# Moving the last weight sums of a seven-product matmul stage, and raising one pair of scan products by a place

## The chip, the cores and the metric

The kernel runs on one core of one Trainium2 chip. A core has TensorE (PE, with its weight loads shown apart as PEld), VectorE (DVE), ScalarE (ACT), GpSimd (POOL) and SyncE (SP, which here only issues transfers). The metric is the device time of one execution in microseconds; lower is better. The kernel before took 369.37 us (median of three executions, 368.46 to 369.98). The profiled execution took 368.5 us, and its profile spans 366.8 us; all points of time below are counted from the start of that span.

## The reference

Two blocks follow each other: a chunked state-space scan, and a feed-forward block with an ELU. Cut to what matters here:

```
# scan: x (4, 8, 768, 32), a (4, 8, 768), B and C (4, 8, 768, 16), float32
for c in range(24):                           # chunks of 32 tokens
    y_intra = (C B^T * decay, causal) @ x     # inside the chunk
    y_inter = (C @ state) * decay_to_i        # from earlier chunks
    state   = decay_full * state + sum_j B_j x_j decay_from_j
# bridge: (batch, head, token, d) -> 3072 tokens x 256
h = y @ w_in                                  # 256 -> 2048
g = where(h > 0, h, exp(min(h, 0)) - 1)       # ELU
out = g @ w_out                               # 2048 -> 256
```

## The kernel before, in words

**Blocks.** The 3072 tokens are cut into 12 blocks of 256, numbered n = 0 to 11 in the order of work. The scan of a block ends with products from earlier chunks (`across`, L522) and inside a chunk (`inside`, L542); ScalarE copies their result into `yT`, the left factor of the first feed-forward layer. Two blocks can go through `across` and `inside` together; the table `ends` (L959) says at which step of which block that happens, and `end_of_two` (L961) does it and then calls `sum_y`.

**Blocks 0 to 3** go one at a time. `l1(n, i)` (L577) is one eighth i of the first layer, `l2(n, j)` (L696) one eighth of the second. `elu` (L598) is two passes of ScalarE (L596, L603) and one of VectorE (L605) on a 128x512 tile. For block 3, eighth i, the loop emits, in this order: `l2(1, i)`, `end_of_two(3, 2i)`, `l1(3, i)`, `elu`, one eighth of the weights' sums, `scan_ahead`, `end_of_two(3, 2i+1)`.

**Blocks 4 to 11** go two at a time with a scheme of Strassen's kind: seven products of half size and some sums take the place of eight products, in both layers. It needs sums ahead of the products:

- sums of the weights: `sum_weights` (L621), four `tensor_tensor` of 128x128 per eighth and layer, all recorded as L627. `more_sums(i)` (L1010) does eighth i: the four of `w_out` on VectorE, the four of `w_in` on GpSimd, and `sum_t1(2, i)` (L721, recorded as L723), a subtraction on 128x256 between the two blocks' activations, on VectorE. Before the change, `more_sums(0)` to `more_sums(6)` stand in eighths 1 to 7 of block 3, and `more_sums(7)` stands in the second group of the stage below.
- sums of the scan's results: `sum_y(n)` (L641, recorded as L646), four subtractions on 128x256 on GpSimd, one reading another's result.
- sums of the activations for the second layer: `sum_t2` (recorded as L719) and the subtractions inside `second` (also L719), on GpSimd.

**A stage by two blocks** is a loop over 16 half steps k, i = k // 2; here called eight *groups* i = 0 to 7. The stage of blocks 4 and 5 carries the second layer of blocks 2 and 3 along in `steps = second(2)`, a generator of 56 steps, one 128x128x256 product each; `l2s(c)` takes c of them. The order on TensorE's queue in a group is:

```
front(n, i)        3 products   L651; ACT copies the first one (L661)
l2s(2), l2s(2)     4 products   L753
mid(n, i)          2 products   then DVE L678 reads the second one
l2s(2)             2 products
back(n, i)         2 products   the first writes where L678 has read
l2s(1)             1 product
```

`front_sums` (L669, L670), the sum of `mid` (L678) and those of `back` (L685, L686) are 128x256 sums on VectorE; then two `elu` of the group follow. VectorE and GpSimd also collect the second layer's results whenever four of its products are done: `add` in `second` (L745). At the end of its fourth sum (r == 3) GpSimd forms `p5 = p5 + u`; at the end of the fifth (r == 4, the 20th step, in the third group) VectorE adds that p5 to a product. `scan_ahead` puts work for the next two blocks between: in the stage of blocks 4 and 5 two masks of GpSimd (L444, `affine_select`) in the second group and two in the third, and `turn` with `turn_exp` (four transposes on TensorE, L381 and L389 on VectorE) after the third and the fourth group.

The order is written out by hand (`manual_schedule`): every engine executes its instructions in the order in which the program emits them. Tiles come from rotating pools (seven PSUM banks of pool `ps_a`, one of `ps_o`).

Of the kernel before, what the change touches and what calls it, by code (L numbers as in the profile page):

```python
# [28 lines left out]
def kernel(  # L29
# [27 lines left out]
    nc = tc.nc  # L57
# [29 lines left out]
    for k in range(4):  # L87
        (nc.scalar if k % 2 else nc.sync).dma_start(
            out=la0[BH * k:BH * (k + 1)],
# [142 lines left out]
    for v in range(2):  # L232
        nc.gpsimd.affine_select(
            out=low16[Q * v:Q * v + Q], in_=low16[Q * v:Q * v + Q], pattern=[[1, Q]],
# [5 lines left out]
        out=hmask, in_=hmask, pattern=[[-N, NH]], compare_op=ALU.is_ge, fill=0.0,  # L240
        base=0, channel_multiplier=1)
    nc.gpsimd.affine_select(
        out=hmask, in_=hmask, pattern=[[N, NH]], compare_op=ALU.is_ge, fill=0.0,
# [8 lines left out]
        out=minus, in0=ident, scalar1=-1.0, scalar2=None, op0=ALU.mult)  # L252
# [178 lines left out]
    def decay(n, q):  # L431

        decay_of(n, 2 * q)
        decay_of(n, 2 * q + 1)
# [142 lines left out]
    def l1(n, i):  # L577

        ps = psum([P, 2, BLK], "ps_h")
        for j in range(2):  # L580
            m = 2 * i + j
            for k in range(KC):
                nc.tensor.matmul(  # L583
                    out=ps[:, j], lhsT=w_in[:, k, m * P:(m + 1) * P],
                    rhs=yT[n // 2][:, k, n % 2].rearrange("p u i -> p (u i)"),
                    start=(k == 0), stop=(k == KC - 1))
        lag.append((n, i, ps))
# [31 lines left out]


    def sum_weights(eng, a, s, i):  # L621
        a11, a12, a21, a22 = (part[:, i] for part in a)
        s2, s3, s4 = (part[:, i] for part in s)
        for out, in0, in1, op in (
                (s3, a11, a21, ALU.subtract), (a21, a21, a22, ALU.add),
                (s2, a21, a11, ALU.subtract), (s4, a12, s2, ALU.subtract)):
            eng.tensor_tensor(out=out, in0=in0, in1=in1, op=op)  # L627

    def weight_sums():
        return [conv.tile([P, MC // 2, P], F32, tag="w64", name="w_sum", bufs=W_AHEAD)  # L630
# [3 lines left out]
    a_in = a11, a12, a21, a22 = [w_parts[:, k, r] for r in range(2) for k in range(2)]  # L634
    w_parts = w_out.rearrange("p (i k) (r c) -> p k r i c", k=2, c=P)
    a_out = [w_parts[:, k, r] for r in range(2) for k in range(2)]
    s_in, s_out = [], []
# [12 lines left out]
    def part_product(out, lhsT, rhs, first=False):  # L650
        nc.tensor.matmul(  # L651
            out=out, lhsT=lhsT, rhs=rhs, start=first, stop=True, skip_group_check=True)
# [27 lines left out]
    def back(n, i):  # L680
        c1, c2, u = open_.pop((n, i))
        b22 = yT[n // 2][:, 1, 1].rearrange("p u i -> p (u i)")
        part_product(c1[:, 1], a22[:, i], y_sums[n][:, 3])
        part_product(c2[:, 0], s_in[2][:, i], b22)
        nc.vector.tensor_tensor(out=c1[:, 1], in0=c1[:, 1], in1=u[:, 0], op=ALU.add)  # L685
        nc.vector.tensor_tensor(out=c2[:, 0], in0=c2[:, 0], in1=u[:, 0], op=ALU.add)  # L686
        lag.append((n, i, c1))
        lag.append((n + 1, i, c2))
# [7 lines left out]
    def l2(n, j, half=None):  # L696


        if j == 0 and half != 1:
            o_of[n] = p_o.tile([P, 2, DM], F32, tag="o", name="ps_o")  # L700
        for m in (2 * j, 2 * j + 1) if half is None else (2 * j + half,):
            for ts in range(2):
                nc.tensor.matmul(  # L703
                    out=o_of[n][:, ts], lhsT=g_of[n, j][:, m % 2, ts * P:(ts + 1) * P],
                    rhs=w_out[:, m], start=(m == 0 and ts == 0), stop=(m == MC - 1),
                    skip_group_check=True)
        if j == MC // 2 - 1 and half != 0:
            ob = ffn.tile([P, 2, DM], F32, tag="ob", name="ob")
            nc.scalar.copy(out=ob, in_=o_of.pop(n))
            r0 = row_of(n)  # L710
            nc.sync.dma_start(
                out=out[r0:r0 + BLK, :].rearrange("(t p) e -> p t e", p=P), in_=ob)
# [5 lines left out]
    def sub(out, in0, in1):  # L718
        nc.gpsimd.tensor_tensor(out=out, in0=in0, in1=in1, op=ALU.subtract)  # L719

    def sum_t1(n, i, eng=nc.gpsimd):  # L721
        b12 = g_of[n + 1, i][:, 0]
        eng.tensor_tensor(out=b12, in0=b12, in1=g_of[n, i][:, 0], op=ALU.subtract)  # L723

    def sum_t2(n, half):
        for i in range(4 * half, 4 * half + 4):
            t2_of[n, i] = ffn.tile([P, BLK], F32, tag="t2", name="t2", bufs=4)
            sub(t2_of[n, i], g_of[n + 1, i][:, 1], g_of[n + 1, i][:, 0])
# [80 lines left out]
    def w_take(i, low):  # L809

        w_abs(i)
        w_low(i, low)
        w_sign(i)

    def w_give(i):

        w_high(i)
        w_sum(i)
# [137 lines left out]

    ends = {(3, 14): (4, 5), (4, 12): (6, 7), (6, 12): (8,), (6, 14): (9,), (8, 13): (10, 11)}  # L959

    def end_of_two(n, step):  # L961
        ns = ends.get((n, step))
        if ns:
            inside(across(*ns), *ns)
            if ns[-1] % 2:
                sum_y(ns[-1] - 1)
# [43 lines left out]
    def more_sums(i):  # L1010
        sum_weights(nc.vector, a_out, s_out, i)
        sum_weights(nc.gpsimd, a_in, s_in, i)
        sum_t1(2, i, nc.vector)


    for n in (2, 3):
        for i in range(8):
            l2(n - 2, i)
            if todo < len(pieces):
                w_take(todo, nc.vector)  # L1020
            end_of_two(n, 2 * i)
            l1(n, i)
            if todo < len(pieces):
                w_give(todo)
                w_load(todo + 6)
                todo += 1
            while lag:
                elu()
            if n == 2:
                if i < 2:  # L1030
                    decay(3, 2 * i)
                    decay(3, 2 * i + 1)
                if i == 1:
                    scaled(3, nc.gpsimd)
                    turn(3)
                    turn_exp(3)
                if i == 2:
                    scores(3)
                    for q in range(4):
                        weigh(3, q)  # L1040
                if i == 4:
                    sums(3)
                    states(3)
                if i == 6:
                    inside(across(3), 3)
            else:
                if i == 0:
                    s_in[:], s_out[:] = weight_sums(), weight_sums()
                else:
                    more_sums(i - 1)  # L1050
            scan_ahead(n, i)
            end_of_two(n, 2 * i + 1)
    sum_t2(2, 0)

    for n in range(4, NP, 2):
        m = n + 2 if n + 2 < NP else None
        steps = second(n - 2)

        def l2s(count):
            for _ in range(count):  # L1060
                next(steps)

        def next_elu():
            if lag:
                at = lag[0][:2]
                elu()
                if at[0] % 2:
                    sum_t1(at[0] - 1, at[1])

        for k in range(16):  # L1070
            i = k // 2
            if k % 2 == 0:
                if m and i == 5:
                    l2s(3)
                    next_elu()
                    weigh_two(m, 1)
                    sums(m, m + 1)
                    front(n, i)
                    weigh_two(m, 2)
                    front_sums(n, i)  # L1080
                    weigh_two(m, 3)
                else:
                    front(n, i)
                    front_sums(n, i)
                    next_elu()
                    if n == 4 and i == 1:
                        more_sums(7)
                    l2s(2)
                    end_of_two(n, k)
                    l2s(2)  # L1090
            elif m and i == 5:
                l2s(2)
                mid(n, i)
                states(m)
                l2s(2)
                back(n, i)
                states(m + 1)
                next_elu()
                begin_elu()
            else:  # L1100
                mid(n, i)
                if i == 0 and n > 4:
                    store(n - 4, turn_out(n - 4, 0))
                    store(n - 3, turn_out(n - 4, 1))
                l2s(2)
                back(n, i)
                l2s(1)
                next_elu()
                begin_elu()
            if m:  # L1110
                scan_ahead(n + k // 8, k % 8)
                if k == 9:
                    scores(m, m + 1)
                    weigh_two(m, 0)
                if k % 2:
                    end_of_two(n, k)
        for _ in steps:
            pass
    next_elu()

    n = NP - 2
# [50 lines left out]
```

## Time and profile before

| engine | busy us | share of the span |
|---|---|---|
| PE (matmul) | 355.7 | 97% |
| PEld (weight load) | 299.3 | 82% |
| DVE | 244.8 | 67% |
| POOL | 226.4 | 62% |
| ACT | 207.0 | 56% |

The granted TensorE clock was 1.000 over the whole span. "Busy" of PE contains modelled ends of pipelined matmuls, so what TensorE loses is better read from gaps in front of its weight loads. In the stages in question a product of 128x128x256 shows as two weight loads and two matmuls; two such products advance the queue by 0.86 us, so one is worth 0.43 us. The whole seam between block 3 and the third group of the first stage by two lies between 107 and 140 us, and the lines on it are shown with the prediction.

### The profile page before, as it was taken

The page shows a single profiled execution, that of the slowest core. Times are in us where ns is not written, and L with a number is a line of the kernel's source. Part 1 is how long each engine was busy: PE and PEld are TensorE (multiplying, and loading weights), DVE is VectorE, ACT ScalarE, POOL GpSimd, SP SyncE. Part 2 cuts the span into 40 slices and gives each one's busy share as a digit, 9 for nine tenths or more (in the row PEclk, how much of TensorE's full clock was granted, in tenths as well). Part 3 has the DMA queues.
Part 4 walks back from the last instruction along what each step waited for, and adds up shares of the span by engine and source line. Part 5 has one row for each costly group of instructions (what it writes and reads, how often), then busy time and mean ns, then how long its engine had stood idle before and what let it go on. Part 6 is the DMA issues. An engine that isn't in the chain of part 4 may idle for free.

```text
span 366.8 us, 9144 instructions
## 1 busy us (share of the span) xinstructions
PE 355.7 (97%) x3458; PEld 299.3 (82%) x3458; DVE 244.8 (67%) x550; ACT 207.0 (56%) x515; POOL 226.4 (62%) x364
## 2 busy tenths in 40 slices
PE   8899999999999889999999999999999999999995
PEld 5578878888888778788888778888888888888884
DVE  3989978972795777785567784566784566656212
ACT  4859969766336466644686645486735452535101
POOL 4454544654376886679366678558579545464972
PEclk9999999999999999999999999999999999999999
DMA  8979895561053430063260063151000010000101
GB/s 152 229 198 224 218 243 140 61 126 33 3 116 57 57 61 1 5 122 39 66 92 2 3 119 43 45 86 30 2 2 2 22 37 0 3 0 0 61 0 57
DMA packets 96252, 25.27 MB, mean 69 GB/s; under 512 B 77328, under 2 KB 92112, under 8 KB 96208
## 3 DMA queue, kind: packets, MB, share of 16 engines
q1 hardware_dynamic: 94032, 24.49, 32.2%
q8 instruction: 27, 0.44, 0.5%
q10 hardware_dynamic: 2176, 0.20, 0.4%
q14 instruction: 17, 0.14, 0.1%
HBM read 21.33 MB, written 3.34 MB: 67 GB/s over the span
## 4 chain that ended last, share of the span: by engine, by line
PE 87%; DVE 7%; ACT 2%; POOL 1%; issue 1%; DVEq 0%; POOLq 0%; ACTq 0%
PE ps_o L753 31%; PE ps_h L651 25%; PE ps_h L583 14%; PE ps_o L703 8%; PE ps_y L553 2%; PE ps_g L459 2%; PE ps_t L796 1%; PE ps_y L534 1%; DVE g L605 1%; PE ps_st L489 1%; PE ps_idle L215 1%; ACT e L596 1%; DVE mag L183 1%; DVE mag L190 1%; ACT e L603 1%
## 5 line engine op out<-in xcount | busy, mean ns | idle before, releaser
L596 ACT ACTIVATE e<-ps_h 128x512 f32<-128x512 f32 x96 | 56.4, 588 | 87.8 <-DVE ps_h L685 66.6
L605 DVE SCALAR_TENSOR_TENSOR g<-e,ps_h 128x512 f32<-128x512 f32 x96 | 65.2, 682 | 41.7 <-ACT e L603 41.6
L753 PE MATMUL ps_o<-g,w_out 128*128 128x256 f32 x320 | 79.6, 380 | 0.0
L753 PEld LDWEIGHTS ps_o<-g,w_out 128*128 128x128 f32 x320 | 60.2, 190 | 8.5 <-issue 0.5
L723 POOL TENSOR_TENSOR g<-g 128x256 f32<-128x256 f32 x32 | 23.3, 727 | 69.3 <-DVE g L605 69.3
L583 PE MATMUL ps_h<-yT,w_in 128*128 128x256 f32 x256 | 60.7, 383 | 2.3 <-ACT w_in L164 1.4
L603 ACT ACTIVATE e<-e 128x512 f32<-128x512 f32 x96 | 60.9, 634 | 2.1
L583 PEld LDWEIGHTS ps_h<-yT,w_in 128*128 128x128 f32 x256 | 47.7, 190 | 10.5 <-POOL w_in L200 3.0
L753 PE MATMUL ps_o<-g,w_sum 128*128 128x256 f32 x160 | 42.1, 380 | 0.0
L651 PE MATMUL ps_h<-y_sum,w_in 128*128 128x256 f32 x128 | 38.6, 383 | 2.7 <-DVE ps_h L678 2.6
L439 ACT ACTIVATE L<-L,ncum 128x64 f32<-128x64 f32 x160 | 41.0, 338 | 0.0
L651 PE MATMUL ps_h<-y_sum,w_sum 128*128 128x256 f32 x128 | 38.5, 382 | 0.4 <-DVE g L605 0.2
L651 PE MATMUL ps_h<-yT,w_in 128*128 128x256 f32 x128 | 38.5, 382 | 0.0
L444 POOL TENSOR_SCALAR_AFFINE_SELECT L<-L 64x512 f32<-64x512 f32 x40 | 27.4, 685 | 12.6 <-ACT L L439 11.3
L753 PEld LDWEIGHTS ps_o<-g,w_sum 128*128 128x128 f32 x160 | 30.2, 190 | 4.3 <-DVE g L605 0.2
L703 PE MATMUL ps_o<-w_out,g 128*128 128x256 f32 x128 | 30.7, 382 | 0.0
L651 PEld LDWEIGHTS ps_h<-y_sum,w_in 128*128 128x128 f32 x128 | 23.5, 189 | 7.9 <-DVE ps_h L678 3.1
L719 POOL TENSOR_TENSOR g<-t,g 128x256 f32<-128x256 f32 x40 | 27.8, 729 | 1.1 <-PE ps_o L753 1.1
L719 POOL TENSOR_TENSOR t<-g 128x256 f32<-128x256 f32 x40 | 28.1, 735 | 0.3
L651 PEld LDWEIGHTS ps_h<-y_sum,w_sum 128*128 128x128 f32 x128 | 23.9, 190 | 5.1 <-issue 0.9
L719 POOL TENSOR_TENSOR g<-g,t 128x256 f32<-128x256 f32 x40 | 27.8, 725 | 0.2
L685 DVE TENSOR_TENSOR ps_h<-ps_h,u_sum 128x256 f32<-128x256 f32 x32 | 13.7, 430 | 20.4 <-PE ps_h L651 20.3
(114 smaller groups left out, 558.1 us busy)
## 6 DMA issues: line engine op xcount, KB each, us to landing
L<-flat SPq DMA_DIRECT2D x20, 256.0 KB, 4.6
w<-in_moe_w_in_dram SPq DMA_DIRECT2D x8, 512.0 KB, 5.0
w<-in_moe_w_out_dram SPq DMA_DIRECT2D x8, 512.0 KB, 6.3
xr<-in_x_dram SPq DMA_DIRECT2D x24, 128.0 KB, 3.6
out_dram<-ob SPq DMA_DIRECT2D x11, 256.0 KB, 2.2
bc<-in_B_dram SPq DMA_DIRECT2D x24, 64.0 KB, 3.9
bc<-in_C_dram SPq DMA_DIRECT2D x22, 64.0 KB, 3.3
ec<-flat_exp SPq DMA_DIRECT2D x72, 16.0 KB, 1.7
```

Source lines behind the costliest of these rows:

```text
L439: nc.scalar.activation(L[:, h, u], L[:, h, u], ACT.Exp, bias=ncum[:, u, row:row + 1])
L444: nc.gpsimd.affine_select(out=part, in_=part, pattern=[[0, 4], [0, 2], [1, Q]], compare_op=ALU.is_ge, fill=0.0, base=0, channel_multiplier=-1)
L583: nc.tensor.matmul(out=ps[:, j], lhsT=w_in[:, k, m * P:(m + 1) * P], rhs=yT[n // 2][:, k, n % 2].rearrange("p u i -> p (u i)"), start=(k = ...
L596: nc.scalar.activation(begun[0], lag[0][2], ACT.Relu, scale=-1.0)
L603: nc.scalar.activation(e, e, ACT.Exp, scale=-1.0)
L605: nc.vector.scalar_tensor_tensor(out=g_of[n, i], in0=e, scalar=1.0, in1=ps, op0=ALU.subtract, op1=ALU.max)
L651: nc.tensor.matmul(out=out, lhsT=lhsT, rhs=rhs, start=first, stop=True, skip_group_check=True)
L685: nc.vector.tensor_tensor(out=c1[:, 1], in0=c1[:, 1], in1=u[:, 0], op=ALU.add)
L703: nc.tensor.matmul(out=o_of[n][:, ts], lhsT=g_of[n, j][:, m % 2, ts * P:(ts + 1) * P], rhs=w_out[:, m], start=(m == 0 and ts == 0), stop=( ...
L719: nc.gpsimd.tensor_tensor(out=out, in0=in0, in1=in1, op=ALU.subtract)
L723: eng.tensor_tensor(out=b12, in0=b12, in1=g_of[n, i][:, 0], op=ALU.subtract)
L753: nc.tensor.matmul(out=ps, lhsT=a[:, i], rhs=b, start=(i == chunk[0]), stop=(i == chunk[-1]))
```

## The change

It does three things, all around that seam.

1. `inside(across(4, 5))` with `sum_y(4)` stood at step 14 of block 3, between `l2(1, 7)` and `l1(3, 7)`. It is put at step 13, so at the end of eighth 6, ahead of `l2(1, 7)`. The sums that the first group needs are to be ready when it starts.
2. `more_sums(6)` leaves the end of block 3, and `more_sums(7)` leaves the second group. VectorE's eight sums of `w_out` for these two eighths (four each) are handed out two at a time behind `back` in each of the groups 0, 1, 2 and 3.
3. GpSimd's four sums of `w_in` for eighth 6 come behind `back` of group 0, those of eighth 7 behind `back` of group 1. `sum_t1(2, 6)` and `sum_t1(2, 7)` go with them, on GpSimd where they were on VectorE.

No arithmetic is added or dropped.

```
     def sum_weights(eng, a, s, i):
+        for step in weight_steps(eng, a, s, i):
+            step()
+
+    def weight_steps(eng, a, s, i):
...
-            eng.tensor_tensor(out=out, in0=in0, in1=in1, op=op)
+            yield lambda: eng.tensor_tensor(out=out, in0=in0, in1=in1, op=op)
...
-    ends = {(3, 14): (4, 5), (4, 12): (6, 7), (6, 12): (8,), (6, 14): (9,), (8, 13): (10, 11)}
+    ends = {(3, 13): (4, 5), (4, 12): (6, 7), (6, 12): (8,), (6, 14): (9,), (8, 13): (10, 11)}
...
                 if i == 0:
                     s_in[:], s_out[:] = weight_sums(), weight_sums()
-                else:
+                elif i < 7:
                     more_sums(i - 1)
...
     sum_t2(2, 0)
+    left = (step for i in (6, 7) for step in weight_steps(nc.vector, a_out, s_out, i))
...
                     next_elu()
-                    if n == 4 and i == 1:
-                        more_sums(7)
                     l2s(2)
...
                 back(n, i)
+
+                if n == 4 and i < 4:
+                    for _ in range(2):
+                        next(left)()
+                    if i < 2:
+                        sum_weights(nc.gpsimd, a_in, s_in, 6 + i)
+                        sum_t1(2, 6 + i)
                 l2s(1)
                 next_elu()
                 begin_elu()
```

## The prediction

> **What bounds the kernel now.** TensorE. On the page's first part PE is busy 355.7 of 366.8 us, and its part 4, the chain that ended last, begins:
>
> ```profile
> PE 87%; DVE 7%; ACT 2%; POOL 1%; issue 1%; DVEq 0%; POOLq 0%; ACTq 0%
> ```
>
> So a change is worth what it takes out of TensorE's queue or out of its waits. The next view is busy time by stretches (columns: stretch and its length, then PE, PEld, DVE, ACT, POOL busy, clock, DMA share, GB/s). I cut it where the weight load of each group's `front` starts, so the rows are groups 0 to 3 of the stage of blocks 4 and 5:
>
> ```profile
> 116.70:124.64 7.94, 6.55 (x29) 5.16 (x28) 5.14 (x11) 1.91 (x5) 7.51 (x13) 1.00 0.48 52
> 124.64:132.37 7.73, 6.32 (x30) 5.24 (x29) 5.85 (x14) 4.77 (x14) 5.94 (x10) 1.00 0.49 75
> 132.37:138.41 6.04, 6.04 (x29) 5.31 (x28) 4.12 (x10) 4.40 (x13) 5.24 (x9) 1.00 0.23 36
> 138.41:144.94 6.53, 6.53 (x33) 5.63 (x32) 4.71 (x12) 4.67 (x14) 4.96 (x8) 1.00 0.00 1
> ```
>
> Group 2 is the undisturbed one: 14 products in 6.04 us, 0.43 us each. Row 4 contains about 0.5 us of transposes and otherwise the same 6.0. Groups 0 and 1 exceed 6.04 by 1.90 and 1.69 us, **3.59 us together**. The weight-load timeline says where (in brackets the idle time ahead and its releaser):
>
> ```profile
> 117.67 0.30 PEld L651 LDWEIGHTS ps_h<-y_sum,w_sum 128*128 128x128 f32 x2 [0.56 <-POOL y_sum L646]
> ...
> 123.45 0.30 PEld L651 LDWEIGHTS ps_h<-y_sum,w_in 128*128 128x128 f32 x2 [1.60 <-POOL t L719]
> ...
> 131.18 0.30 PEld L651 LDWEIGHTS ps_h<-y_sum,w_in 128*128 128x128 f32 x2 [1.82 <-DVE ps_h L678]
> ```
>
> The first is `front(4, 0)` waiting for `sum_y`. The second and third are `back` of groups 0 and 1. The matmul of the second waits on DVE L678 (its own record says 1.23 us for that), the POOL name being only the last event seen. They add up to 3.98 us; the groups lost 3.59, since loads after a gap follow closer (0.32 us instead of 0.43). I use 3.59. VectorE's timeline shows why L678 is late in group 0:
>
> ```profile
> 118.41 0.69 DVE L605 SCALAR_TENSOR_TENSOR g<-e,ps_h 128x512 f32<-128x512 f32 x1 [3.73 <-ACT e L603]
> 119.01 0.54 DVE L627 TENSOR_TENSOR w_sum<-w_out 128x128 f32<-128x128 f32 x1
> ...
> 121.06 0.94 DVE L723 TENSOR_TENSOR g<-g 128x256 f32<-128x256 f32 x1
> 121.93 0.41 DVE L669 TENSOR_TENSOR u_sum<-ps_h,p_copy 128x256 f32<-128x256 f32 x1
> ...
> 122.91 0.43 DVE L678 TENSOR_TENSOR ps_h<-ps_h,u_sum 128x256 f32<-128x256 f32 x1
> ```
>
> `more_sums(6)` stands ahead of `front_sums`, from 119.01 to 121.93. In group 1 `more_sums(7)` does the same from 128.09 to 130.38.
>
> **What the Trainium skill says.** "PSUM — Partial Sum Buffer", section Engine vs sequencer instructions: the queues of ScalarE, VectorE and GpSimd are strict FIFO. The trace agrees: L669 had its input at 118.63 and started at 121.93, when the sums ahead of it were done. "SBUF — State Buffer", section Who interferes with whom: a VectorE instruction with two SBUF inputs contends with a GpSimd one that reads SBUF. The trace agrees: an L627 on VectorE takes 0.28 us at 128.09 with GpSimd idle and about 0.50 beside its sums. "Perfetto Trace Analysis", section GPSIMD Engine Instruction: time GpSimd by the spacing of starts. L627 there lasts 0.45 us by its record, but starts come 0.53 apart; I use spacings.
>
> **The change, part by part.**
>
> *Scan products up.* On TensorE only the order changes, cost nothing. `l2(1, 7)` is 8 loads, 1.73 us (110.77 to 112.5), so `inside`, the copies of `yT` and `sum_y` come 1.73 us earlier. The second result of `sum_y` was used at 117.67; 1.73 earlier is 115.9, ahead of 117.1 where TensorE asks. The 0.56 us gap closes. The copy of block 1's output, now behind the `yT` copies, ends near 115.9 instead of 113.5; the bank is needed at 118.0 and the transfers queued behind it on SP are used after 134, so nothing waits.
>
> *Sums out of VectorE ahead of L678.* With `front(4, 0)` at 116.70 undisturbed: 3 products to 118.0, 4 to 119.7, `mid` to 120.6, L678 ready at 121.0. VectorE has L605 to 119.0, L669 and L670 to 120.0, so it is waiting there. In group 2 L678 ends (137.10) just where `back` wants to start (137.16): there is no slack, and any lateness of VectorE is a gap on TensorE. Here there is none; both long gaps close.
>
> *Two sums behind each `back`.* After L686 VectorE waited 0.89, 0.90 and 1.00 us for ACT (groups 0 to 2) and 0.47 in group 3. Two L627 at 0.45 to 0.50 fill 0.9 to 1.0, so L605 is late by 0.1 at most in groups 0 to 2. In groups 1 and 2 VectorE stands 0.35 to 0.4 us ahead of L678. In group 3 the excess of 0.1 to 0.5 meets 0.42 us of idle time ahead of the next L678. Cost: nothing on the path.
>
> *GpSimd.* The same eight L627, and two L723 at 0.69 spacing that VectorE did in 0.41 and 0.94. They now stand in the middle of the stage's GpSimd work, while TensorE comes earlier. Two lines of before are the measure:
>
> ```profile
> 136.74 0.72 POOL L745 TENSOR_TENSOR p_sum<-p_sum 128x256 f32<-128x256 f32 x1
> ...
> 137.60 0.42 DVE L745 TENSOR_TENSOR c_sum<-ps_o,p_sum 128x256 f32<-128x256 f32 x1 [0.50 <-PE ps_o L753]
> ```
>
> The second needs the first and product r == 4; both were there near 137.5. After the change, groups start at 116.70, 122.74 and 128.78, so r == 4 is done at 128.78 + 5.13 = 133.9. GpSimd: `sum_y` to 117.2, four L719 to 120.0, four more from 120.2 to 123.0, eighth 6 (4 x 0.53) to 125.1, L723 to 125.8. The next L723 needs the second `elu` of group 0, which came 3.54 us after the front of group 1, so 126.35. From there without a pause: L723 0.69, four L719 2.77, two masks 1.38, eighth 7 2.1, two L723 1.38, the p5 sum 0.72, together 9.04: 135.4. VectorE gets it at 135.55 instead of 134.0: **late by 1.55 us**. Behind that add on VectorE are L685, L686, the `elu`s, `turn`'s two, `front_sums` and L678 of group 3. Before, VectorE ran without a gap from 140.02 to that L678 at 143.28, where it was already 0.17 us behind the product. Nothing absorbs it: `back` of group 3 waits some 1.55 us, less 0.1 for the closer loads: **1.45 us given back**. After it GpSimd catches up in pauses of 1.43 and 4.24 us (before L723 at 143.10 and 149.41), and the groups from 4 on only move.
>
> *Sum.* 369.37 - 3.59 + 1.45 = **367.2 us**. The unseen resource is the backlog on GpSimd. Its lower bound is zero (365.8). For an upper one, every L627 on GpSimd at its longest 0.72 instead of 0.53 adds 8 x 0.19 = 1.5: 368.7. I take the middle, for which I have every duration.
>
> **Rivals.** *All of it comes in, 365.8 us*: GpSimd keeps up, group 3 runs in 6.5. For it: its pauses of before (1.55 us at 126.7) are filled first. Against: the 9.04 us run above fits in no way into the 7.5 us from 126.35 to 133.9. *Half of the likely gain, 368.4 us*: port conflicts stretch two L627 behind each `back` from 0.9 to 1.4 us (0.71 was seen once), VectorE misses L678 by 0.1 to 0.2 in groups 1 and 2, and GpSimd's lag grows by 0.8; together 1.2 more. For it: VectorE and GpSimd overlap much more here. *Slower, 370.1 us*: the bound becomes GpSimd for the whole first half, and a 1.45 us wait comes back in three groups, 4.35 in all against 3.59 gained, 0.76 net. Against: pauses in groups 3 and 4 sum to 5.67 us.
>
> **How the numbers follow.** Likely case 0.50, full gain 0.25, half 0.17, slower 0.08. Faster by over 0.5% means below 367.52: about 0.7 of the first case (0.35), all of the second, little of the third (0.03): 0.63. Within: 0.15 + 0.13 + 0.02 = 0.30. Slower 0.07. Runs of before scatter by 0.7 us around the median. With that, 365.3 to 368.8 reaches to both neighbouring cases and leaves out the slower one and the edges.
>
> **What would show it.** In the profile after: no PEld wait on L646 and none over 0.2 us on L678 in groups 0 and 1, which are 6.0 us long; L627 of VectorE in pairs between L686 and L605; the DVE L745 of r == 4 waiting for POOL L745; group 3 some 1.5 us longer, its `back` waiting for L678. I am wrong if group 3 stays at 6.5 us (then 365.8), or if L678 is late in groups 1 and 2 too.

## The result, and the profile after

The changed kernel took **365.81 us** (median of 4 executions, 365.62 to 366.49) against 368.99 us of the kernel before measured along with it: ratio **0.9914, 95% interval 0.9888 to 0.9941**, 2.2 to 4.1 us faster. Its profile spans 363.9 us instead of 366.8. The new helper shifts all later lines by four: what was L627, L678, L685, L723, L745 before is L631, L682, L689, L727, L749 after.

The page's part 4, the chain that ended last:

```profile
PE 90%; DVE 6%; ACT 1%; POOL 1%; issue 1%; DVEq 0%; POOLq 0%; ACTq 0%
```

Busy time by stretches, cut at the same instructions as before (columns: stretch and length, then PE, PEld, DVE, ACT, POOL busy, clock, DMA share, GB/s):

```profile
115.97:122.02 6.05, 6.05 (x30) 5.25 (x29) 2.33 (x6) 1.86 (x4) 6.05 (x10) 1.00 0.67 103
122.02:128.06 6.04, 6.04 (x30) 5.31 (x28) 4.39 (x11) 4.78 (x14) 4.89 (x9) 1.00 0.52 57
128.06:134.10 6.04, 6.04 (x29) 5.31 (x28) 4.53 (x9) 4.40 (x13) 5.66 (x11) 1.00 0.64 101
134.10:142.06 7.96, 7.02 (x33) 5.54 (x32) 6.41 (x16) 4.67 (x14) 6.56 (x10) 1.00 0.01 3
```

The lengths are the reading: groups 0 and 1 fell from 7.94 and 7.73 us to 6.05 and 6.04; the row of group 3 rose from 6.53 to 7.96. From the front of group 0 to the front of group 4, which I call *the seam*, it is 26.64 us (115.97 to 142.61) where it was 28.79 (116.70 to 145.49): 2.15 us less. From there to the end both profiles need 221.3 us. The other 0.73 us between the two spans lies ahead of the first changed instruction, and the experiments come back to it.

The weight-load timeline of groups 0 to 3 has two waits left, both in group 3:

```profile
138.18 0.30 PEld L655 LDWEIGHTS ps_h<-yT,w_in 128*128 128x128 f32 x2 [0.65 <-ACT p_copy L665]
...
140.88 0.30 PEld L655 LDWEIGHTS ps_h<-y_sum,w_in 128*128 128x128 f32 x2 [1.10 <-DVE ps_h L682]
```

The first is `mid`, waiting for ScalarE's copy, the second `back`, waiting for VectorE's L682. Where VectorE lost its time shows on GpSimd's timeline, at the p5 sum, and on its own:

```profile
133.97 0.72 POOL L749 TENSOR_TENSOR p_sum<-p_sum 128x256 f32<-128x256 f32 x1
```

```profile
132.36 0.43 DVE L682 TENSOR_TENSOR ps_h<-ps_h,u_sum 128x256 f32<-128x256 f32 x1
134.72 0.42 DVE L749 TENSOR_TENSOR c_sum<-ps_o,p_sum 128x256 f32<-128x256 f32 x1 [1.93 <-PE ps_tb L374]
...
140.40 0.42 DVE L682 TENSOR_TENSOR ps_h<-ps_h,u_sum 128x256 f32<-128x256 f32 x1
```

VectorE stands still for 1.93 us ahead of the add of r == 4 and starts it 0.03 us after GpSimd's p5 sum ends (133.97 + 0.72). The name in the bracket, a transpose of TensorE, is only the last event before; the add doesn't read it. A releaser's name has to be held against what the instruction reads. From the add at 134.72 to L682 at 140.40 the profile shows no further wait of VectorE, so `back` of group 3 is late by what the add is late.

### The profile page after: what moved, and what is told of

Same layout as the page of the kernel before. It is cut to its first block, busy times and chain, and to the rows that moved or that the text cites. A ratio compares the mean times of both kernels' runs of the same rounds, so it can differ in the third digit from the quotient of the medians.

```text
span 363.9 us, 9138 instructions
## 1 busy us (share of the span) xinstructions
PE 354.9 (98%) x3458; PEld 299.1 (82%) x3458; DVE 243.5 (67%) x548; ACT 207.0 (57%) x515; POOL 227.5 (63%) x366
## 4 chain that ended last, share of the span: by engine, by line
PE 90%; DVE 6%; ACT 1%; POOL 1%; issue 1%; DVEq 0%; POOLq 0%; ACTq 0%
PE ps_o L757 32%; PE ps_h L655 26%; PE ps_h L583 14%; PE ps_o L707 8%; PE ps_y L553 2%; PE ps_g L459 2%; PE ps_t L800 1%; PE ps_y L534 1%; PE ps_st L489 1%; PE ps_idle L215 1%; DVE g L605 1%; DVE mag L183 1%; DVE mag L190 1%; PE ps_tb L374 1%; PE ps_tc L374 1%
## 5 line engine op out<-in xcount | busy, mean ns | idle before, releaser
L727 POOL TENSOR_TENSOR g<-g 128x256 f32<-128x256 f32 x34 | 24.7, 727 | 67.7 <-DVE g L605 67.7
L723 POOL TENSOR_TENSOR g<-t,g 128x256 f32<-128x256 f32 x40 | 27.8, 728 | 1.1 <-PE ps_o L757 1.1
L723 POOL TENSOR_TENSOR t<-g 128x256 f32<-128x256 f32 x40 | 28.0, 732 | 0.2
L723 POOL TENSOR_TENSOR g<-g,t 128x256 f32<-128x256 f32 x40 | 27.9, 728 | 0.3
L689 DVE TENSOR_TENSOR ps_h<-ps_h,u_sum 128x256 f32<-128x256 f32 x32 | 13.8, 430 | 20.4 <-PE ps_h L655 20.4
```

## The experiments

The ten experiments were each timed in five rounds beside the kernel before on the same chip (e1 to e4 on one, e5 to e7 on a second, e8 to e10 on a third), and each leaves a profile. Two measures are given: the ratio of the times, and the seam in the profile. Of the same kernel the seam comes out the same within 0.02 us, so it is the finer one for anything that happens inside it. It is blind to what happens behind it: from the front of group 4 to the kernel's last two loads of a transpose (L796 before, L800 after) TensorE needs 217.25 to 217.28 us in eight of the twelve profiles, but 217.32 in e5, 217.36 in e8, 217.52 in e6 and 217.55 in e7. The groups in the table run from front to front, so group 2 contains the transposes (6.59 us undisturbed).

| kernel | groups 0, 1, 2, 3, us | seam, us | median, us | ratio (95% interval) |
|---|---|---|---|---|
| before | 7.94, 7.73, 6.59, 6.53 | 28.79 | 368.99 | 1 |
| changed | 6.05, 6.04, 6.59, 7.96 | 26.64 | 365.81 | 0.9914 (0.9888 to 0.9941) |
| e1: scan products up, alone | 8.42, 7.73, 6.58, 6.53 | 29.26 | 369.87 | 1.0032 (1.0019 to 1.0044) |
| e2: sums moved, alone | 6.47, 6.04, 6.59, 8.46 | 27.56 | 367.94 | 0.9966 (0.9953 to 0.9980) |
| e3: GpSimd's sums later | 6.04, 6.04, 6.59, 6.65 | 25.32 | 365.71 | 0.9912 (0.9893 to 0.9932) |
| e4: changed, again | 6.04, 6.04, 6.59, 7.96 | 26.63 | 367.15 | 0.9949 (0.9932 to 0.9967) |
| e5: p5 sum on VectorE | 6.05, 6.04, 7.00, 6.48 | 25.57 | 366.41 | 0.9913 (0.9885 to 0.9941) |
| e6: no pair in group 2 | 6.04, 6.04, 6.59, 7.96 | 26.63 | 367.47 | 0.9947 (0.9928 to 0.9965) |
| e7: e3, no pair in group 1 | 6.04, 6.05, 6.58, 6.84 | 25.51 | 366.50 | 0.9929 (0.9902 to 0.9957) |
| e8: e3, no pair in groups 1, 2 | 6.04, 6.05, 6.58, 6.54 | 25.21 | 365.70 | 0.9900 (0.9870 to 0.9930) |
| e9: e3, again | 6.04, 6.05, 6.58, 6.67 | 25.34 | 365.90 | 0.9904 (0.9873 to 0.9935) |
| e10: changed, a third time | 6.05, 6.04, 6.59, 7.97 | 26.65 | 367.55 | 0.9939 (0.9921 to 0.9958) |

The kernel before, timed along with e1 to e4, e5 to e7 and e8 to e10, had medians of 368.95, 369.18 and 369.40 us.

### The parts one by one (e1, e2)

e1 is the kernel before with one edit:

```
-    ends = {(3, 14): (4, 5), ...
+    ends = {(3, 13): (4, 5), ...
```

> The kernel before, with the scan products of blocks 4 and 5 one place up and nothing else. Theory of the chain: L678 of group 0 ends at a time that VectorE sets (second elu of block 3 at 118.4, then 2.9 us of weight sums, then front_sums), so closing the 0.56 us gap at sum_y only makes the gap ahead of back longer by as much. Groups 0 and 1 stay at 15.6 to 15.7 us from the front of group 0 to that of group 2, total within 0.3 us of before (ratio 0.999 to 1.001). Rival, parts that add up: the gap at sum_y is worth its own 0.45 to 0.56 us, total 0.5 us less than before (ratio 0.9986).

Measured: seam 29.26 us, 0.47 *longer* than before, and 0.3% slower. The gap at `sum_y` is gone, as expected; the next gap takes it and more. Its weight-load line for `back` of group 0, and two of VectorE's sums ahead of L678:

```profile
125.61 0.30 PEld L651 LDWEIGHTS ps_h<-y_sum,w_in 128*128 128x128 f32 x2 [2.51 <-POOL g L719]
```

```profile
121.14 0.70 DVE L627 TENSOR_TENSOR w_out<-w_out 128x128 f32<-128x128 f32 x1
121.87 0.70 DVE L627 TENSOR_TENSOR w_sum<-w_out 128x128 f32<-128x128 f32 x1
```

The gap grew from 1.60 to 2.51 us, by 0.91. Some 0.43 of that is the closed gap, net of the closer loads behind it, as expected: VectorE and not TensorE sets the end of L678. The other 0.48 comes from VectorE itself: three of its four sums take 0.70 us here instead of 0.49 to 0.50, because GpSimd, released earlier, is by now in its 128x256 subtractions (four from 120.92) instead of its short sums; the stretch from the first sum to L669 is 3.40 us instead of 2.92. That this is GpSimd's doing rests on the times lying side by side and on the same slowing in other places; no run changes GpSimd alone here. My expected 0.3 us bound was broken; the rival, a gain of 0.5, is ruled out. The ratio puts the loss at 1.2 us (0.7 to 1.6), more than the seam does. The new order on TensorE isn't the rest: from the last `l1` ahead of the moved products to the front of group 0 it needs 7.65 us, and 7.66 before. The rest stays open.

e2 is the changed kernel with that edit undone.

> The changed kernel, with the scan products of blocks 4 and 5 put back to step 14. Theory of the chain: the gap of 0.56 us at sum_y in group 0 comes back (0.45 net), and GpSimd starts its run 1.7 us later, which the pauses of GpSimd ahead of the L723 of group 0 take up but for about 0.4, so that the p5 sum comes 0.4 us later against TensorE and group 3 grows by as much: 0.85 us slower than the changed kernel, some 1.3 us of gain left by the seam. Rival, parts that add up: 0.45 us slower than the changed kernel. Other rival, the early scan products do nothing: same as the changed kernel.

Measured: seam 27.56 us, 0.92 more than the changed kernel (0.85 expected): 0.42 in group 0, where the gap of 0.56 us at `sum_y` is back, and 0.50 in group 3, where the p5 sum ends 7.13 us after the front of group 2 (6.63 in the changed kernel). Ratio 0.9966, a gain of 1.25 us; 1.23 by the seam. So the scan products' move is worth 0.92 us with the sums moved and -0.47 without. The larger half of the 0.92 isn't at the gap that it closes; it comes from GpSimd's earlier start, paid out three groups later.

### What makes group 3 long (e3, e5, e6)

e3 moves only GpSimd's weight sums, out of groups 0 and 1:

```
                     if i < 2:
-                        sum_weights(nc.gpsimd, a_in, s_in, 6 + i)
                         sum_t1(2, 6 + i)
+                    else:
+                        sum_weights(nc.gpsimd, a_in, s_in, 4 + i)
```

> The changed kernel, with GpSimd's sums of w_in for the last two eighths behind back of groups 2 and 3 instead of groups 0 and 1; the two sums of activations stay. This takes 4.2 us from GpSimd ahead of the p5 sum. Theory that the p5 sum is late: it now starts as soon as its inputs are there, the VectorE add of r == 4 waits 0.2 us at most for it, both gaps in group 3 (0.65 and 1.10 us of weight-load idle in the changed kernel) close, group 3 goes from 7.96 back to about 6.5 us, total 1.4 us less than the changed kernel (364.4). Rival, the two extra VectorE sums behind back are what makes L678 late in group 3: group 3 stays near 7.9 us and the total at 365.8.

Measured: group 3 6.65 us instead of 7.96, seam 1.32 us shorter than that of the changed kernel (1.4 expected). Total 365.71 us against 367.15 of the changed kernel on the same chip, 1.44 less. The rival falls. VectorE's add still waits for p5, but the line now names GpSimd and a third of the time:

```profile
134.82 0.42 DVE L749 TENSOR_TENSOR c_sum<-ps_o,p_sum 128x256 f32<-128x256 f32 x1 [0.62 <-POOL p_sum L749]
```

Most of those 0.62 us are TensorE's. In the kernel before, where the add waited 0.50 us for its product, it started 5.23 us after the front of group 2 (137.60 - 132.37). Here it starts 5.36 us after it (134.82 - 129.46), so p5 holds it for 0.13 us, less than the 0.2 expected. One short wait of 0.30 us on L682 is left in group 3.

e5 leaves GpSimd's load alone and takes the p5 sum from it:

```
-                    add(p5, p5, u)
+                    if n == 2 and not half:
+                        nc.vector.tensor_tensor(out=p5, in0=p5, in1=u, op=ALU.add)
+                    else:
+                        add(p5, p5, u)
```

> The changed kernel, with the p5 sum of the third group on VectorE (0.42 us) instead of GpSimd; GpSimd's load ahead of it is left as it is. Theory that VectorE's add of r == 4 waits for GpSimd: it now starts at 133.3 instead of 134.7 (as counted in the changed kernel), group 3 falls from 7.96 to 6.5 or 6.6 us, while the extra 0.42 us ahead of L678 of group 2 costs 0.2 to 0.5 us there. From the front of group 0 to that of group 4 25.4 to 25.7 us against 26.64. Rival, GpSimd's load slows VectorE through the shared port, whoever does the p5 sum: group 3 stays above 7.5 us and the total at that of the changed kernel.

Measured: group 3 6.48 us, group 2 7.00 (0.41 more), seam 25.57, all as expected. The rival falls. On VectorE the sum took 0.67 us beside GpSimd's sums, and L682 of group 2 came that late:

```profile
134.53 0.67 DVE L776 TENSOR_TENSOR p_sum<-p_sum 128x256 f32<-128x256 f32 x1
135.12 0.42 DVE L682 TENSOR_TENSOR ps_h<-ps_h,u_sum 128x256 f32<-128x256 f32 x1
```

```profile
135.59 0.30 PEld L655 LDWEIGHTS ps_h<-y_sum,w_in 128*128 128x128 f32 x2 [0.55 <-DVE ps_h L682]
```

With e3 this shows the cause from two sides: relieve GpSimd ahead of the p5 sum, or take the sum off GpSimd, and group 3 is short again, with the same sums done in the same stage.

e6 takes VectorE's pair out of group 2 and puts it behind `back` of group 4.

> The changed kernel, with no VectorE pair of weight sums behind back of group 2; the pairs go behind back of groups 0, 1, 3 and 4. Theory: the pair lies beside ScalarE's two passes and costs nothing, group 3 stays at 7.9 to 8.0 us, from front of group 0 to front of group 4 26.6 us. Rival, the pair makes L678 of group 3 late: group 3 falls to 7.0 us or less, as the pair took 1.0 us there.

Measured: 7.96 us for group 3, seam 26.63, no change; the rival falls. The line of the first `elu` behind `back` of group 2 shows what the pair had stood in:

```profile
139.19 0.69 DVE L605 SCALAR_TENSOR_TENSOR g<-e,ps_h 128x512 f32<-128x512 f32 x1 [0.99 <-ACT e L603]
```

Without the pair VectorE waits 0.99 us for ScalarE there; with it, it works for 1.02 and waits for nothing. In group 2 the pair was free, as costed.

In its new place behind `back` of group 4, past the end of the seam, it was not:

```profile
150.91 0.59 DVE L631 TENSOR_TENSOR w_sum<-w_out 128x128 f32<-128x128 f32 x1
151.53 0.70 DVE L631 TENSOR_TENSOR w_sum<-w_out,w_sum 128x128 f32<-128x128 f32 x1
152.16 0.68 DVE L605 SCALAR_TENSOR_TENSOR g<-e,ps_h 128x512 f32<-128x512 f32 x1
```

It took 1.25 us (150.91 to 152.16) where VectorE waits 0.89 us for ScalarE in the changed kernel. TensorE comes to the second product of the front of group 5 10.56 us after the front of group 4 instead of 10.31, and keeps this 0.25 us to the end. Of the other profiles only e7, which has a pair in this place too, is late there by as much (10.61).

### How much is the gain (e4, e9, e10)

> The changed kernel once more, unaltered, for the size of the gain. From the front of group 0 to that of group 4 the profiles give 28.79 us before and 26.64 after, 2.15 us; the rest of the 2.9 us between the two profiled spans lies ahead of the first changed instruction (0.44 us ahead of 20 us, 0.28 near 51 us). Theory that this rest is scatter of the start: the ratio comes out at 0.993 to 0.995 (1.8 to 2.6 us), and the front of group 0 varies by some tenths from run to run. Rival, it belongs to the change: ratio 0.991 to 0.992 again (2.9 us or more) and the front of group 0 at 116.0 again.

> The kernel with GpSimd's weight sums behind back of groups 2 and 3, once more, unaltered. If the length from front of group 0 to front of group 4 is what the change decides, it is 25.3 us again, and the ratio to before lies 0.003 to 0.004 below that of the changed kernel on the same chip. If its first 365.7 us were luck of the start, the two come out alike.

> The changed kernel a third time, unaltered, beside the two above. Theory: 26.6 us from front of group 0 to front of group 4 again, ratio 0.993 to 0.996 (gain 1.5 to 2.6 us), the front of group 0 anywhere between 116 and 119 us. Rival: ratio 0.991 as in the first measurement.

Measured: the changed kernel's ratio comes out at 0.9949 and 0.9939, gains of 1.9 and 2.3 us (0.0051 x 368.95 and 0.0061 x 369.40); e6, with the same seam, gives 0.9947. The 0.991 of the rivals did not come again, and the seam says 2.15. The first measurement's 0.9914 (3.2 us) rests on four executions. Its interval includes 0.9939 but not 0.9949, and the interval of e4 reaches up to a gain of 2.5 us. The front of group 0 was at 115.97 us in the profile of the first measurement, 118.74 in e4's and 118.02 in e10's, with the same instructions ahead of it. That is far more than the tenths that I expected. From there to the end the three profiles need the same, 247.9 us (363.9 - 115.97 in the first), and the granted clock (0.999, 1.000 and 0.995) doesn't order them. Over all 12 profiles the front lies between these ends, in no order that follows the kernels. In the changed kernel's first profile the 0.73 us that it is ahead of the kernel before came in two pieces: the weight loads of L410 (32 of them) took 0.46 us instead of 0.75 and began 0.14 earlier, and near 51 us a wait ahead of weight loads was 0.33 instead of 0.60. What sets the start apart from run to run was not followed further. So the likely size of the change is the seam's, 2.15 us, and I put 1 us of the first measured 3.2 down to start and scatter.

e9 repeats e3: seam 25.34, ratio 0.9904 beside 0.9939 of the changed kernel, 1.3 us apart by ratio and by seam alike.

### Towards a better version (e7, e8)

e7 is e3 with VectorE's pairs behind `back` of groups 0, 2, 3 and 4.

> GpSimd's weight sums behind back of groups 2 and 3 (as in the experiment that did this alone), and VectorE's pairs behind back of groups 0, 2, 3 and 4, none in group 1, where the pair took 1.45 us beside GpSimd's masks. Theory: the second elu of group 1 then ends about 0.4 us earlier, the p5 sum on GpSimd, which waits for the L723 behind that elu, too, and the last wait on L678 in group 3 (0.27 us of weight-load idle) closes: from front of group 0 to front of group 4 25.1 us against 25.32 of that experiment and 26.64 of the changed kernel. Rival, L678 of group 3 is late from VectorE's own work behind it: 25.3 us again.

This one did not bring what was expected. The p5 sum came in time, as expected (VectorE's add waits 0.50 us for TensorE, as in the kernel before), but group 3 took 6.84 us, 0.2 more than in e3. Now that VectorE was on time, its pair of group 2 fell beside GpSimd's work:

```profile
135.26 0.75 DVE L631 TENSOR_TENSOR w_sum<-w_out 128x128 f32<-128x128 f32 x1
136.04 0.70 DVE L631 TENSOR_TENSOR w_sum<-w_out,w_sum 128x128 f32<-128x128 f32 x1
```

The pair took 1.41 us instead of 1.02, in a place that holds 1.0. Of the 0.4 us too much, 0.3 arrived at TensorE: `back` waited 0.49 us for L682, and 0.18 in e8 below, where no pair stands in group 2 (0.30 in e3). Behind the seam the pair in group 4 costs another 0.3 us, as in e6. That a pair costs nothing is true only while it fits into ScalarE's two passes.

e8 is e3 as well, and puts four of VectorE's sums ahead of the last `elu` of block 3, where it stood idle for 3.24 us, and the other four behind `back` of groups 0 and 3:

```
+            if n == 3 and i == 7:
+                for _ in range(4):
+                    next(left)()
             while lag:
                 elu()
...
-                    for _ in range(2):
+                    if i in (0, 3):
+                        next(left)()
                         next(left)()
```

> GpSimd's weight sums behind back of groups 2 and 3, and VectorE's pairs out of groups 1 and 2: four sums (eighth 6) go ahead of the last elu of block 3, where VectorE waited 3.24 us for TensorE, the other four in pairs behind back of groups 0 and 3. Theory: pairs cost nothing only where the wait for ScalarE behind them is not filled by GpSimd's port use; with none in groups 1 and 2 the p5 sum and L678 of group 3 are both on time. Groups 6.04, 6.04, 6.59 and 6.50, from front of group 0 to front of group 4 25.2 us (25.32 with the sums only moved on GpSimd, 25.51 with pairs in groups 0, 2, 3 and 4). Rival, the four sums in block 3 delay sum_y on GpSimd through the port and reopen the gap in group 0: group 0 at 6.3 us or more.

Measured: groups 6.04, 6.05, 6.58, 6.54, seam 25.21 as expected, ratio 0.9900, 365.70 us. The four sums took 2.5 us beside `sum_y` and still ended ahead of the `elu`, so the rival falls. Against e3 it is 0.11 us by the seam, and TensorE loses 0.10 us of that again behind it (217.36 against 217.26 us), so e8 is no better than e3. e3, e8 and e9 all beat the changed kernel by 1.3 to 1.4 us of seam.

## Why the prediction was right or wrong

**Where the kernel lost time: right.** The 3.59 us of excess in groups 0 and 1 went as costed, to 6.05 and 6.04 us.

**Scan products up, 0.56 us: right as part of the whole only.** The gap closed. Alone the edit makes the seam 0.47 us longer (e1); next to the sums it is worth 0.92 (e2), because it starts GpSimd earlier. The prediction counted the gap and not this second part, which sits inside its GpSimd sum.

**Pairs behind `back` at nothing: right where it mattered, its size off.** The pair in group 2 took 1.02 us and cost nothing (e6). The pair in group 1 took 0.86 and 0.62 us beside GpSimd's subtractions and masks, 1.45 in all and not 0.9 to 1.0. VectorE stood 0.43 us ahead of L678 of group 2 before and 0.13 ahead of L682 now (132.23 to 132.36), so most of the slack that the prediction named was used up; L682 still started as early as the product before it allows. The rule behind it is the Trainium skill's "SBUF — State Buffer", Who interferes with whom: a VectorE instruction with two inputs in SBUF contends with a GpSimd instruction that reads SBUF. The profiles agree: 0.28 us for such a sum alone, about 0.50 beside short sums of GpSimd, and mostly 0.6 to 0.9 beside its longer work (0.70 in e1, 0.70 and 0.75 in e7).

**GpSimd late by 1.55 us, 1.45 given back: right.** Group 3 grew by 1.43 us. The p5 sum ended 134.69 - 128.06 = 6.63 us after the front of group 2; the prediction had 135.4 - 128.78 = 6.6. e3 and e5 show this to be the cause. The size has a little luck in it. The add followed the p5 sum by 0.03 us where 0.15 was allowed, so it was late by 1.43 (6.66 us after the front of group 2 instead of 5.23) and not by 1.55. The 0.1 us taken off for closer loads was not there to take, because this load had stood behind a wait before as well:

```profile
143.75 0.30 PEld L651 LDWEIGHTS ps_h<-y_sum,w_in 128*128 128x128 f32 x2 [0.18 <-DVE ps_h L678]
```

The two slips all but cancel. Missed was that the loss shows in two waits, of `mid` (0.65 us) and of `back` (1.10). ScalarE's timeline of the changed kernel has the first:

```profile
135.85 0.60 ACT L596 ACTIVATE e<-ps_h 128x512 f32<-128x512 f32 x1 [3.34 <-DVE ps_h L689]
...
137.75 0.39 ACT L665 COPY p_copy<-ps_h 128x256 f32<-128x256 f32 x1
```

ScalarE's first pass waited for L689 behind the late add, and the copy of `front`'s first product stands behind that pass in ScalarE's queue; `mid` writes where this copy reads, and its load came at 138.18, after the copy's end at 138.14. The Trainium skill's "PSUM — Partial Sum Buffer", Engine vs sequencer instructions, calls ScalarE's queue strict FIFO as well; I had walked down VectorE's only. The sum is the same, as both waits hang on one late add and VectorE, not `mid`, sets the end of L682.

**The total, 367.2 us: inside its range, off by 1.4 us from the first measurement.** The step that is off is none of the stage's: the seam's gain was predicted as 3.59 - 1.45 = 2.14 and is 2.15. The predicted 367.2 is 0.994 of the 369.37 us it starts from; the changed kernel's later ratios are 0.9949 and 0.9939, its times 367.15 and 367.55 us. The start, which the prediction took as common to both kernels, differs by up to 2.8 us between profiles of the changed kernel alone.

**The rivals.** Full gain, 365.8: the time of the first measurement agrees with it and the mechanism doesn't, since group 3 gave 1.43 us back; agreement of a total is no proof of a story. Half gain: a pair did stretch to 1.45 us, in group 1, but no load waited for L682 in groups 1 and 2, and GpSimd's lag was as costed. Slower: GpSimd's backlog ended in group 3, where it paused 1.19 us ahead of its L727, and in group 4 it paused 4.23.

## What to carry to other kernels

When work is moved off the engine that makes the bound wait, follow the queue that takes it in, instruction by instruction, to the next place where another engine reads from it: here 4.2 us of sums that TensorE reads in groups 6 and 7 stood ahead of one sum of 0.72 us that was due at once, and their order on GpSimd cost 1.4 of 3.6 us gained. Put work without a near deadline behind the sums that are waited for, and check its slot against its duration beside the neighbour engine, not alone. For a change of half a per cent compare a stretch between two fixed instructions in the profiles; it repeated to 0.02 us where totals scattered by more than the effect. Then see that nothing is lost behind that stretch: e6 looked free in it and lost 0.25 us later.

## What was not expected of the hardware

A 128x128 float32 sum of two SBUF operands on VectorE took 0.28 us alone and up to 0.88 us beside GpSimd (e5), three times as long; 128x256 sums with one operand in PSUM stayed at 0.41 to 0.43 us in all these places. The way to the front of group 0 took the changed kernel 115.97, 118.74 and 118.02 us in three profiles.
